# A second filter spectrum folded on VectorE out of PSUM, products on VectorE alone, GELU buffers by product slice and q in small loads

## The chip, the cores and the metric

The kernel runs on one core of a Trainium2 chip. A core has five engines with a queue each, and each works through its queue in the order written: TensorE (PE; its weight loads are shown apart as PEld), VectorE (DVE), ScalarE (ACT), GpSimd (POOL) and SyncE (SP), which here issues all the DMA transfers. The metric is the device time of one execution in microseconds. Before the change it is 228.35 us, the median of 3 runs (228.15 to 230.0).

## The reference

Two blocks follow one another on 2048 rows of 512 features, in bf16. Block A is a gated long convolution along the rows, block B a local mix and an MLP.

```python
x = A_q
h  = x + _A_ref(_layernorm(x), A_k, A_v, A_shift_k, A_ssm_k, A_ssm_D)
h2 = h + _B_ref(_layernorm(h), B_w1, B_w2, B_w3, B_w4)

# A: kv = (4-tap causal filter of k) * v
#    y  = irfft(rfft(kv padded to 4096) * rfft(ssm_k padded to 4096))[:2048]
#    A  = q * (y + kv * ssm_D)
# B: h  = gelu(layernorm(x) @ w1); its four quarters shifted by -1, +1, -2, +2 rows; @ w2
#    x1 = x + that;  B = x1 + gelu(layernorm(x1) @ w3) @ w4
```

## The kernel before

The convolution is done as a transform of 4096 points on TensorE, in two halves of 1024 rows. Signals are F0 and F1 (the filter's first half, and the whole filter for the second half of the rows) and A0 and A1 (the two halves of kv). The kernel is a list of small tasks. Each is made with `add(name, ...)` and knows its operands; a table `ORDER` (line 30) was written by a planner and says for each task its place, its engine (letter P, V, A, G or S) and the buffers it takes. `Plan.emit` (line 85) walks through the table, so each engine's queue is in the table's order. A wait at the head of a queue holds all that is behind it.

The tasks that matter, with their lines (S, h and p stand for a half, a part and a pair of row blocks):

- K, KV (lines 456, 457): the 4-tap filter on TensorE with diagonal matrices `dg` made of the taps, then times v out of PSUM on VectorE (L449).
- S1, E1, X (line 403): the forward transform's first step (L397), its eviction out of PSUM as a cast of 1024 columns (L266) and eight exchanges through SBUF to SBUF DMAs (L412). F1 sums two sources in PSUM, `fb` (the filter's second half) and `f0` (its first half with another table, `f1b`).
- S2, E2 (line 424): the second step (L420) and its eviction, the spectrum. E2 is a cast of 1024 columns on ScalarE or VectorE.
- P, I2, EV, XI (line 464): four or eight products for each of four slices `kl` of a half (L473, 1024 columns, two SBUF inputs), on VectorE or GpSimd, with four buffers; the inverse step (L485), its eviction and exchange (L495). The second half takes A0 x F1 and A1 x F0.
- I1 (line 499): the last inverse step (L503).
- Q, QN (lines 507, 516): mean and variance of q's rows (L512, L513), the reciprocal root as a power on GpSimd.
- Y, H, HS (line 580): normalised q, h (L591), h's statistics. uw, rr, hn (line 598) turn them into scale and bias.
- hb, LT, TE, W, U (line 653): normalised h, its transposition on TensorE or by two DMAs (`BYDMA`; a write and a DMA transpose), times w1 (L672), GELU (L676).
- X2, S, SS, R (line 683): the shifted product with w2 (L701), x1 (L704), its statistics, the rest (L708).
- lb, LX, EX, M, G, O, Z, OUT (line 715): normalised x1, transposition, times w3 (L752), GELU (L756), times w4 (L765), sum (L767) and store.

The GELU's outputs have three buffers `gb` (line 155) in memory of kv and of A1's spectrum. All G but those of the first pair of blocks wait for every product of A1 x F0 (line 759).

Of the kernel before, what the change touches and what calls it, by code (L numbers as in the profile page):

```python
# [9 lines left out]
P = 128  # L10
# [6 lines left out]
XW = 258  # L17

# [12 lines left out]
023V 004S 021P7 022P 055P01 001S 057P23 005S 061P45 006S 028V 029V 031V 032G 056A 008S 062A 058A 011S 059P67 060A 000S 024V 030A 091P10 033V 092V 002S  # L31
027V 003S 095P5 096V 083P41 034G 038V 039V 049P01 047P23 048A 035G 053P67 009S 050A 007S 054A 097P5 098V 093P3 014S 010S 084V 085P2 087P7 094V 040A
025A 109P01 036V 037A 086V 051P45 052A 089P6 017S 107P23 088V 111P45 041G 042V 043A 046G 067S 110V 108A 090V 045G 016S 070S 113P01 019S 114A 112V
099P67 103P23 104A 013S 101P45 102A 105P01 100V 063S 071P6723 072A 065S 073A 106V 333V 069S 211P50 212V 335V 064S 077P0167 079A 119S 026V 121S 078A
068S 115S 217P4 218V 123P2367 124V 125A 066S 080P0145 136V0 082A 135V1 116S 081A 213P7 120S 126P2345 127A 139G2 214V 128V 074P0167 076A 117S 015S 075V
138V3 129P2345 131A 130A 137P67010 122S 140P 012S 189P45 118S 177P23 141A 190A 179P67 337V 178A 018S 180A 175P45 176A 145V0 142V 143S 144V1 147V2
148V3 146P01231 149P 332V 151A 150A 183P67 153V0 020S 338V 181P45 182A 193S 192S 184V 336V 154G1 152S 156V2 185P23 186A 187P01 188A 132P4567 133A 194S
339V 157G3 334V 196S 219P31 134A 340G 191S 221P2 155P01450 158P 220V 044A 223P3 159A 222V 163V0 162V1 166V2 165V3 215P2 216V 160A 341G0 344G1 197S
164P67011 167P 168A 169V 229P45 224V 331G 195S 225P2 230A 226V 199P0167 200V 263V0 201A 233P45 234A 198S 241P23 161S 264G1 237P67 238A 235P01 236A
421V 170S 171P54 239P67 417V 242A 231P01 345V 232A 342V 347G0 240V 330S 422V 208P2345 343A 209A 172P10 210A 227P67 350G1 351V 356G1 173P32 348V 353G0  # L40
352V 228A 357V 346A 354V 365G 349A 174P54 362V1 363V 205P0167 207A 247S 366G 243S 206A 249S 359V0 360V 202P2367 204A 203A 251P0167 252A 367V 368V0
371V1 244S 267V2 253A 248S 266V3 378G 379G 380G 245S 369P50 372P4 370A 373V 254P0123 255V 256A 246S 381G0 265P67450 268P 384G1 364A 361A 257P0123 258A
269V0 259A 270V1 272V2 271P 382P11 385P0 403G 327S 273V3 274P 404G 405G 383A 328S 276A 374P3 275A 279V0 358A 250S 278V1 386V 375A 376P2 282V2 377A
355A 391G 407V0 392G 281V3 280P01451 283P 260P6723 409S 393G 261A 406V1 285V0 284V1 287V2 277S 288V3 286P 262A 408S 410S0 294V0 289P 290A 389P7 390A
293V1 387P6 295P01230 297V2 296V3 291A 298P 394V0 396S 395V1 397S 388A 299V0 413P7 414A 300V1 411P6 412A 302V2 303V3 301P 419V 304P 501P7 292S 306A
305A 309V0 308V1 502V 497P6 498V 503A 499A 311V2 561G 312V3 398S0 401P5 402A 420V 399P7 310P01231 314V0 313P 315V1 317V2 562G 400A 307S 563G 564A0
567A1 505P7 506V 507A 509P6 318G3 510V 418V 517P5 565P40 566V 513P7 568P6 569A 316P 329S 319P 511V 590G 320A 415V 591G 321A 570P60 571A 514V 416V 423G
592V 593A0 580P4 322S 595S 594A1 596S 515A 581A 576P7 597S1 582P3 574P6 583A 577A 424A0 578P2 572P1 573A 575A 579A 518V 519V 427G1 618G 504V 323P54
428V 324P73 325P10 429A 425V 426A 433G1 434V 619G 439G0 440V 430A1 435A 431V 620G 622A0 624S 326P64 598P51 604P3 599A 610P2 611A 445V0 446V 500V 448G
587P0 441A 436A1 432V 449G 450G 454A0 608P7 437V 588V0 438A 602P2 603A 584P5 621G1 623S 451A1 452P40 473V 474G 475G 453A 455P2 456A 606P1 607A 600P4  # L50
457P2 442G0 601A 625S0 476V1 478S 477V0 479S 480S1 461G 462G 463G 443V 464G1 447V 459P6 605A 465V0 609A 467S 466S 444A 626P40 468S0 632P7 458A 512V
636P3 638P2 485V 486G 460A 521P6 522V 523V 585V1 586S 525P1 639A 487G 488G0 489A1 628P2 481P6 629A 526V 527V 469P0 470A 646V 483P5 484A 630P2 631A
647G 637A 471P1 648V 650A0 649G1 615P5 490S 491S 492S1 495P0 493P3 472A 482A 541P6 494A 537P1 538V 540V 496A 529P3 530V 634P2 545P1 542V 543A 549P3
550V 633A 539A 674G 533P0 627A 553P6 524V 589S 534V 546V 535V 651S 544V 652S 531V 675G 653S1 730V 654P72 731G 612P4 658P3 732V 676G 551A 733G0 554V
547V 702V 735S 734V1 656P1 659A 616V0 528V 557P0 655A 660P3 661A 558V 662P7 677V0 664P6 635A 643P5 736S 737S0 520V 640P0 738P31 657A 536V 679S 665A
666P6 678G1 680S 559A 617S 703G 552V 663A 746P7 747A 704G 706G0 532V 708S 744P2 681S1 555A 644V0 645S 508V 740P5 748P7 758V 759G 760G 613V1 614S 742P1
516V 667A 761V0 682P60 745A 690P4 684P2 683A 705V1 707S 743A 686P6 685A 560V 694P1 762G1 671P2 672V0 673S 741A 750P5 641V1 687A 688P6 689A 764S 739A
691A 695A 668P2 692P6 749A 693A 709S0 710P42 556V 712P3 711A 722P7 763S 751A 765S1 752P6 755P5 716P4 766P11 713A 776P3 642S 777A 778P0 779A 753V0 754S
756V1 757S 699P6 718P5 669V0 670S 772P0 774P3 767A 773A 768P2 775A 770P1 771A 720P3 723A 548V 714P0 696P7 700V0 701S 697V0 769A 783P2 784V1 780P1 785S
698S 781V1 782S 721A 715A 717A 719A 727P7 728V0 729S 724P6 725V1 726S  # L60
# [3 lines left out]
class Plan:  # L64
# [4 lines left out]
    def add(self, name, opts, fn, deps=(), take=(), drop=(), size=0, mode=0, port=""):  # L69
        n = len(self.t)  # L70
        t = dict(n=n, name=name, opts=opts, fn=fn, deps=set(), take=list(take), drop=[], size=size, mode=mode, port=port)
        for d in deps:
            t["deps"].add(self.by[d])
        for d, part, *kind in drop:
            m = self.by[d]
            t["deps"].add(m)
            t["drop"].append((m, kind[0] if kind else self.t[m]["take"][0][0], part))
        self.by[name] = n
        self.t.append(t)
# [5 lines left out]
    def emit(self):  # L85
        for word in ORDER.split():
            t, slots, i = self.t[int(word[:3])], [int(c) for c in word[4:]], 0
            t["eng"], t["got"] = word[3], {}
            for kind, k in t["take"]:
                k = k if k > 0 else -2 * k  # L90
                t["got"][kind] = slots[i:i + k]
                i += k
            t["fn"](word[3], t["got"].get("ps", slots))
# [3 lines left out]
def body(ctx, tc, fx, kt, q, v, sk, sd, w1, w2, w3, w4, out):  # L97
# [20 lines left out]
    r_k = raw("r_k", 2 * DC * NB * 129)  # L118
# [12 lines left out]
    kT = r_k[:].rearrange("p (s c b x) -> p s c b x", s=2, c=DC, b=NB)  # L131
# [23 lines left out]
    gb = [view(r, lo, GS, "p (f x) -> p f x", f=FC) for r, lo in ((r_kv, 0), (r_x, 0), (r_x, GS))]  # L155
# [3 lines left out]
    wup = r_vs[:, 0:D]  # L159
# [4 lines left out]
    f1 = ct("f1", 2, 8, 2, 2, 2, 4)  # L164
# [8 lines left out]
    qst = ct("qst", 4, 6, dt=F32)  # L173
# [14 lines left out]
    ssk = ct("ssk", DC * 4)  # L188
# [15 lines left out]
    vec, pool, act = nc.vector, nc.gpsimd, nc.scalar  # L204
    vec.memset(negpi[:], -3.1415925)
# [3 lines left out]
    u1a, u1b = early(64), [early(64) for i in range(2)]  # L209
# [4 lines left out]
    vec.memset(wup, 0.0)  # L214
# [5 lines left out]
    s1 = early(128, BF16)  # L220
    mk = small("mk", 4, F32)

    def f1u(x):
        vec.scalar_tensor_tensor(out=u1b[x], in0=u1a, scalar=nf[:, 0:1], in1=u1b[x], op0=MUL, op1=ADD)
        vec.tensor_scalar(out=u1b[x], in0=u1b[x], scalar1=4095, scalar2=None, op0=AND)

    def f1s(x):
        act.activation(s1[:, 64 * x:64 * x + 64], u1b[x], ACT.Sin, bias=negpi[:], scale=SC)

    def f1m(x):  # L230
        for i in range(2):
            for j in range(2):
                vec.tensor_scalar(out=f1[:, x, :, i, :, j, :], in0=s1[:, 64 * x:64 * x + 64].rearrange("p (a c k) -> p a c k", a=8, c=2),
                                  scalar1=mk[:, 2 * i + j:2 * i + j + 1], scalar2=None, op0=MUL)
    f1u(0)
    f1s(0)
    vec.tensor_scalar(out=mk[:], in0=l4[:], scalar1=nf[:, 1:2], scalar2=None, op0=OP.is_equal)
    f1m(0)
# [3 lines left out]
    pool.iota(u1b[1].rearrange("p (a c k) -> p a c k", a=8, c=2), pattern=[[0, 8], [1024, 2], [0, 4]], base=2048, channel_multiplier=0)  # L242
# [7 lines left out]
    wf = small("wf", 72, F32)[:].rearrange("p (o b) -> p o b", o=9)  # L250
# [14 lines left out]
    def copy(e, o, i):  # L265
        (act.copy if e == A else vec.tensor_copy)(o, i)  # L266

    def pair(sl, k=0):
        return ps[:, sl[2 * k]:sl[2 * k] + 2, :]
# [12 lines left out]
    for c in range(DC):  # L282
        load(("Lk", 0, c), kT[:, 0, c], kt_r[0, c], size=258)
# [531 lines left out]
```

## Time and profile before

| what | value |
|---|---|
| median of 3 runs | 228.35 us |
| the profiled execution's own time | 229.05 us |
| its span (first to last instruction) | 227.3 us |
| PE busy | 203.9 us, 90% |
| PEld busy | 119.4 us, 53% |
| DVE busy | 142.3 us, 63% |
| ACT busy | 133.9 us, 59% |
| POOL busy | 85.6 us, 38% |
| mean granted TensorE clock | 0.977 |
| DMA | 34.49 MB, mean 152 GB/s |

A share is a mean over the whole span. The kernel has an early part (transforms, products) and a late part (matmuls with w1 to w4), and each view is to be read for them apart. In a list in order of time a line gives the start, the time it took, the engine, the line of the code, the operation with output and inputs, how often it comes in a row, and in brackets how long the engine was idle before and what ended that.

### The profile page before, as it was taken

How to read it: one execution, taken by the hardware profiler on the slowest of the kernel's cores; microseconds unless marked ns; L12 is line 12 of the kernel's file. 1: busy time of each engine (PE TensorE's matmuls, PEld its weight loads, DVE VectorE, ACT ScalarE, POOL GpSimd, SP SyncE). 2: the span in 40 equal slices, each digit the busy share in tenths (PEclk: the TensorE clock that was granted, in tenths of full speed). 3: DMA queues.
4: the chain of work that ended last, by engine and by line, in shares of the span. 5: the costliest groups of instructions: out<-in, count | busy, mean ns of one | idle time of the engine just before them, and what ended most of it. 6: DMA issues, size and time to landing. Idle time of an engine off the chain costs nothing.

```text
span 227.3 us, 5985 instructions
## 1 busy us (share of the span) xinstructions
PE 203.9 (90%) x2403; PEld 119.4 (53%) x2421; DVE 142.3 (63%) x309; ACT 133.9 (59%) x213; POOL 85.6 (38%) x210
## 2 busy tenths in 40 slices
PE   7998669998687965999999999899999999999993
PEld 2453224463123523556765877556668666667441
DVE  7789899899999888399484543088935030410221
ACT  4789868997799974458986747242505243037000
POOL 8724020846378774057685742005432100000000
PEclk9999997999997999699999999999999999999999
DMA  5999985698949144474522362700434053200021
GB/s 175 337 419 385 334 279 195 215 350 280 337 157 335 69 141 92 143 252 169 151 57 44 77 140 72 154 8 0 108 80 113 5 115 69 72 23 0 3 69 46
DMA packets 35229, 34.49 MB, mean 152 GB/s; under 512 B 26753, under 2 KB 28802, under 8 KB 34690
## 3 DMA queue, kind: packets, MB, share of 16 engines
q1 hardware_dynamic: 35202, 34.11, 46.8%
q8 instruction: 19, 0.31, 0.6%
q14 instruction: 8, 0.07, 0.1%
HBM read 13.13 MB, written 5.24 MB: 81 GB/s over the span
## 4 chain that ended last, share of the span: by engine, by line
PE 51%; ACT 7%; DMA 7%; DVE 6%; POOL 3%; issue 2%; DVEq 0%; ACTq 0%; SPq 0%; POOLq 0%
PE ps L765 20%; PE ps L752 19%; PE ps L701 5%; PE ps L672 4%; DMA hnT<-dhb 3%; ACT r_f L266 2%; DVE r_p L473 2%; PE ps L485 2%; ACT junk L575 2%; DMA r_dg<-dlb 1%; DMA dhb<-hbt 1%; ACT r_x L266 1%; DMA dlb<-r_k 1%; ACT r_k L625 1%; DVE r_kv L449 1%
## 5 line engine op out<-in xcount | busy, mean ns | idle before, releaser
L752 PE MATMUL ps<-r_dg,r_k 128*128 128x256 bf16 x448 | 51.5, 273 | 0.2 <-DMA r_dg<-dlb 0.2
L752 PEld LDWEIGHTS <-r_k 128*128 128x128 bf16 x448 | 43.6, 98 | 8.3 <-DMA r_dg<-dlb 0.7
L756 ACT ACTIVATE r_x<-ps 128x512 bf16<-128x512 f32 x35 | 19.5, 601 | 29.2 <-PE ps L752 29.2
L765 PE MATMUL ps<-w4s,r_x 128*128 128x512 bf16 x136 | 31.0, 379 | 0.2
L473 DVE TENSOR_TENSOR r_p<-r_a,r_f 128x1024 bf16<-128x1024 bf16 x28 | 23.4, 874 | 3.7 <-PE ps L485 3.6
L765 PEld LDWEIGHTS <-r_x 128*128 128x128 bf16 x140 | 13.7, 98 | 15.4
L485 PE MATMUL ps<-r_p,ttab 32*32 32x512 bf16 x768 | 18.3, 439 | 2.6 <-DVE r_p L473 2.5
L756 ACT ACTIVATE r_kv<-ps 128x512 bf16<-128x512 f32 x21 | 11.9, 604 | 12.8 <-PE ps L752 12.8
L672 PE MATMUL ps<-hnT,r_v 128*128 128x256 bf16 x128 | 16.0, 280 | 3.5 <-DMA hnT<-dhb 3.5
L765 PE MATMUL ps<-w4s,r_kv 128*128 128x512 bf16 x80 | 18.7, 379 | 0.2
L767 DVE TENSOR_TENSOR r_kv<-ps,r_a 128x512 bf16<-128x512 f32 x4 | 2.8, 692 | 24.7 <-PE ps L765 24.7
L266 ACT CAST r_y<-ps 128x1024 bf16<-128x1024 f32 x18 | 17.3, 1025 | 0.7 <-PE ps L397 0.7
L266 ACT CAST r_x<-ps 128x1024 bf16<-128x1024 f32 x15 | 14.5, 1020 | 4.5 <-PE ps L397 3.4
L473 POOL TENSOR_TENSOR r_p<-r_a,r_f 128x1024 bf16<-128x1024 bf16 x4 | 8.9, 2239 | 20.0 <-PE ps L485 10.7
L266 ACT CAST r_vs<-ps 128x1024 bf16<-128x1024 f32 x14 | 13.7, 1017 | 4.1 <-PE ps L485 4.1
L672 PEld LDWEIGHTS <-r_v 128*128 128x128 bf16 x128 | 12.5, 100 | 6.8 <-DMA hnT<-dhb 3.1
L397 PEld LDWEIGHTS <-f 128*32 128x32 bf16 x320 | 8.5, 101 | 13.3 <-issue 6.1
L441 PE MATMUL ps<-r_dg,r_k 128*128 128x256 bf16 (+3 forms) x107 | 14.7, 284 | 0.6 <-issue 0.3
L676 ACT ACTIVATE r_h<-ps 128x512 bf16<-128x512 f32 x16 | 9.1, 606 | 9.9 <-PE ps L672 9.9
L701 PE MATMUL ps<-r_v,r_h 128*128 128x512 bf16 x59 | 14.6, 380 | 0.3
L266 ACT CAST r_f<-ps 128x1024 bf16<-128x1024 f32 x14 | 13.3, 1016 | 2.2 <-PE ps L420 1.9
L485 PEld LDWEIGHTS <-ttab 32*32 32x32 bf16 x768 | 8.6, 90 | 10.7 <-issue 8.8
(165 smaller groups left out, 330.3 us busy)
## 6 DMA issues: line engine op xcount, KB each, us to landing
r_k<-in_kt_dram SPq DMA_DIRECT2D x8, 258.0 KB, 6.6
r_v<-in_v_dram SPq DMA_DIRECT2D x4, 512.0 KB, 7.0
r_f<-r_x SPq DMA_DIRECT2D x8, 256.0 KB, 3.8
r_q<-in_q_dram SPq DMA_DIRECT2D x2, 1024.0 KB, 7.4
r_a<-r_y SPq DMA_DIRECT2D x8, 256.0 KB, 3.7
r_x<-r_vs SPq DMA_DIRECT2D x4, 512.0 KB, 3.8
r_f<-r_y SPq DMA_DIRECT2D x8, 256.0 KB, 4.7
r_x<-r_y SPq DMA_DIRECT2D x8, 256.0 KB, 2.4
```

Source lines behind the costliest of these rows:

```text
L266: (act.copy if e == A else vec.tensor_copy)(o, i)
L397: nc.tensor.matmul(ps[32 * j:32 * j + 32, sl[hh], :], lhsT=f1t[:, i, 4 * t + 2 * hp + hh, :], rhs=src(2 * b + b0), start=(i == 0), stop=(i ...
L441: nc.tensor.matmul(o[:, (d + j0) * P:(d + j1 + 1) * P], lhsT=kT[:, s, c, bb, x:x + P], rhs=diag[:, c, j0:j1 + 1, :].rearrange("p j x -> p ...
L473: on[e].tensor_tensor(out=prs[:, sl[0], :, :], in0=sp[a][:, kl, t, :, :], in1=gv, op=MUL)
L485: nc.tensor.matmul(ps[c:c + 32, bk[h], :], lhsT=ttab[32 * h:32 * h + 32, 2 * kl + t, 2 if x else xx, 32 * b0:32 * b0 + 32], rhs=prs[32 * h ...
L575: act.activation(junk[:], x, ACT.Square, accum_out=sq[:, i, 1:2])
L672: nc.tensor.matmul(ps[:, sl[0], j * 256:(j + 1) * 256], lhsT=w1s[:, k, m * P:(m + 1) * P], rhs=hnT[:, k_, k, :], start=(k == 0), stop=(k = ...
L676: act.activation(h1T[:, 2 * h:2 * h + 2, 2 * p:2 * p + 2, 1 + P * s:1 + P * s + P], ps[:, got(("W", s, p, h))[0], :].rearrange("p (j b x) ...
L701: nc.tensor.matmul(ps[:, sl[0], :], lhsT=h1T[:, m, bb, x:x + P], rhs=w2s[:, m, :], start=(m == 0), stop=(m == DC - 1))
L752: nc.tensor.matmul(ps[:, sl[0], j * 256:(j + 1) * 256], lhsT=w3s[:, k, fc * P:(fc + 1) * P], rhs=lnT[:, k_, k, :], start=(k == 0), stop=(k ...
L756: act.activation(gb[got(("M", s, p, 0), "gb")[0]][:, 2 * fp:2 * fp + 2, :], ps[:, got(("M", s, p, fp))[0], :].rearrange("p (j x) -> p j x" ...
L765: nc.tensor.matmul(ps[:, sl[0], :], lhsT=gb[k_][:, fc, (b % 2) * P:(b % 2 + 1) * P], rhs=w4s[:, fc, :], start=(fc == 0), stop=(fc == FC - 1))
```

## The change

1. F1's first step takes the second half of the filter alone (`fb`), with the same table as F0. The first half's part is added at the spectrum: a task E2 of F1 is no longer a cast but two VectorE instructions, which add F0's spectrum, real and imaginary parts swapped, to what is in PSUM. The second table (`f1u`, `f1s`, `f1b`) is gone. F1 is loaded in four pieces.
2. Products are on VectorE alone.
3. Four GELU buffers `gb0` to `gb3`, each for two of the eight pairs, in memory of kv, A1's spectrum, and F0's and F1's. G of the pairs 1 to 3 waits for the products of one or two slices `kl`, G of the first for A1's first step, and the rest for none of these.
4. q comes in eight loads of 256 KB instead of two of 1 MB. A row's statistics keep the two partial results of L512; the aggregation (L513) is replaced by seven small instructions for eight blocks (QV), then the power (QP, GpSimd) and two instructions (QN).
5. A cast may be wide: marked M in the table, one ScalarE instruction evicts 2048 columns for two tasks. Three are.
6. The taps come with k, four columns behind each block of 1032; their own load is gone and each `dg` waits for its block of k.
7. The warm-up is twenty matmuls of 128 columns instead of five of 512. Planner costs and sizes are other numbers, and the table ORDER is written anew.

On the engines this gives, before to after: products on GpSimd 5 to 0; E2 of F1 on ScalarE 7 to 0 and on VectorE 1 to 8; hb on VectorE 9 to 4, ScalarE 3 to 9, GpSimd 4 to 3; Y on GpSimd 10 to 12, VectorE 3 to 0, ScalarE 3 to 4; `ftv` from GpSimd to VectorE. In TensorE's order W(0,0,1) stands ahead of S2(F1,1) and of the first I2 of the second half. In VectorE's order all eight Q of the second half stand behind its last product (before, three of them did). In SP's order the first half's four q loads stand ahead of all X(F0).

```diff
@@ emit
+        skip = False
         for word in ORDER.split():
...
-            t["fn"](word[3], t["got"].get("ps", slots))
+            if not skip:
+                t["fn"](word[3], t["got"].get("ps", slots))
+            skip = word[3] == "M"
@@ body: buffers
-    gb = [view(r, lo, GS, "p (f x) -> p f x", f=FC) for r, lo in ((r_kv, 0), (r_x, 0), (r_x, GS))]
+    gbq = [[view(r, lo, 2048, "p (f x) -> p f x", f=8) for lo in (0, 2048)] for r in (r_kv, r_x, r_f0, r_f1)]
+
+    def gb(i, f, n=1):
+        u = f // 8
+        r, z = ((0, u), (1 + u, 0), (1 + u, 1), (3, u))[i]
+        return gbq[r][z][:, f % 8:f % 8 + n, :]
@@ loads
-    load(("Lf", 1), fxs[:, 1, :, :].rearrange("p (g b) d -> p g b d", g=4), fx[1].rearrange("g p (b d) -> p g b d", b=2), size=1024)
+    for b in range(4):
+        load(("Lf", 1, b), fxs[:, 1, 2 * b:2 * b + 2, :], fx[1, b].rearrange("p (b d) -> p b d", b=2), size=310)
...
-        load(("Lq", s), q_sb[:, s], q_r[:, s], size=1024)
+        for g in range(4):
+            load(("Lq", s, g), q_sb[:, s, 2 * g:2 * g + 2, :], q_r[:, s, 2 * g:2 * g + 2, :], size=310)
...
-    add("skf", {V: 0.2}, lambda e, sl: vec.tensor_copy(sskf[:], ssk[:]), ["Lsk"])
+    for c in range(DC):
+        add(("skf", c), {V: 0.17, GP: 0.22, A: 0.22}, lambda e, sl, c=c: copy(e, sskf[:, 4 * c:4 * c + 4], kw[:, 0, c, NB * 129:KW]), [("Lk", 0, c)])
@@ forward2
+                if sig == "F1":
+                    def fold(e, sl, n=n, kl=kl, t=t):
+                        for r, op in ((0, SUB), (1, ADD)):
+                            vec.tensor_tensor(out=sp[sig][:, kl, t, r, :], in0=ps[:, got(n)[2 * t + r], :], in1=sp["F0"][:, kl, t, 1 - r, :], op=op)
+                    add(("E2", sig, kl, t), {V: 1.2}, fold, [("E2", "F0", kl, t)], drop=[(n, t)])
+                    continue
@@ conv
-                        add(("P", s, kl, i, x, t), {V: 0.605, GP: 2.4}, f, [("E2", a, kl, t), ("E2", g, kl, t), "f2", "f1b"] + before, take=[("pr", 1)], port="VG")
+                        add(("P", s, kl, i, x, t), {V: 0.605}, f, [("E2", a, kl, t), ("E2", g, kl, t), "f2"] + before, take=[("pr", 1)], port="VG")
@@ statistics of q
     def qstat(s, b):
...
-            vec.bn_stats(qst[:, i % 4, :], x)
-            vec.bn_aggr(qmv[:, i, :], qst[:, i % 4, :])
+        return lambda e, sl: vec.bn_stats(qst[:, 8 * s + b, :], q_sb[:, s, b, :])
+
+    def qvar(s):
...
+            en.tensor_tensor(out=qnm[:, i], in0=m0, in1=m1, op=ADD)
+            en.tensor_tensor(out=qrs[:, i], in0=m0, in1=m1, op=SUB)
+            en.tensor_tensor(out=qsd[:, i], in0=v0, in1=v1, op=ADD)
...
+    def qpow(s):
+        i = slice(8 * s, 8 * s + 8)
+        return lambda e, sl: pool.tensor_tensor(out=qrs[:, i], in0=qsd[:, i], in1=mhalf[:], op=OP.pow)
@@ F1's sources
-    forward1("F1", [fb, f0], lambda b: ["f1b", ("Lf", 1)] + [("Lf", 0, i) for i in range(4)] + ["dr"], lambda b: [("X", "A0", b // 2, kl) for kl in range(4)])
+    forward1("F1", fb, lambda b: ["f1", ("Lf", 1, b)], lambda b: [("X", "A0", b // 2, kl) for kl in range(4)])
@@ back
-            gd = [("S1", "A1", b, hp) for b in range(4) for hp in range(2)] + (allp(1) if g else [])
+            gd = [] if g >= 4 else [("S1", "A1", b, hp) for b in range(4) for hp in range(2)] if g == 0 else [x for kl in range((1, 2, 2)[g - 1]) for x in allkl(kl)]
```

## The prediction

> **What bounds the kernel now.** I read the stretches of ten microseconds first, because two engines change places as the bound. Columns: stretch, its length, then busy us (and instructions) of PE, PEld, DVE, ACT, POOL, then TensorE clock, DMA share, GB/s.
>
> ```profile
> 20.00:30.00 10.00, 7.21 (x116) 3.04 (x117) 8.89 (x14) 8.60 (x11) 2.74 (x3) 1.00 0.94 349
> 50.00:60.00 10.00, 8.63 (x163) 3.43 (x163) 9.60 (x13) 8.07 (x10) 5.89 (x9) 1.00 0.84 289
> 60.00:70.00 10.00, 6.81 (x96) 2.16 (x91) 9.73 (x27) 9.00 (x14) 6.19 (x17) 1.00 0.62 248
> ...
> 160.00:170.00 10.00, 9.95 (x66) 6.27 (x65) 6.80 (x13) 3.27 (x7) 4.68 (x5) 1.00 0.39 93
> 200.00:210.00 10.00, 9.95 (x75) 7.23 (x74) 0.69 (x1) 4.94 (x11) 0.00 (x0) 1.00 0.04 13
> ```
>
> Early, VectorE is 89 to 97% busy and TensorE has holes; late, TensorE has none. The border is the last product of the second half and its matmuls (I2). TensorE in order of time (start, us, engine, line, operation):
>
> ```profile
> 36.01 4.07 PE L397 MATMUL ps<-r_h,f 128*32 128x512 bf16 x64
> 41.12 3.64 PE L397 MATMUL ps<-r_h,f 128*32 128x512 bf16 x64
> ...
> 104.26 1.14 PE L485 MATMUL ps<-r_p,ttab 32*32 32x512 bf16 x64
> 105.33 6.29 PE L752 MATMUL ps<-r_dg,r_k 128*128 128x256 bf16 x56
> ```
>
> From 105 us to the last matmul's end (223.6, the chain of waits) the five-microsecond stretches leave TensorE only 1.5 us idle. Before 104.26 it is idle some 18 us. In both orders exactly the same tasks stand behind the last I2: 56 M, 16 O, 8 W, 10 X2, 4 I1, 2 LT. So **the end is the start of the last I2 plus about 119.4 us** (223.63 - 104.26), and I forecast that start.
>
> What sets it is VectorE's queue of some 100 us. Its order of time, beside GpSimd's, shows what is hidden there:
>
> ```profile
> 28.02 3.21 DVE L473 TENSOR_TENSOR r_p<-r_a,r_f 128x1024 bf16<-128x1024 bf16 x2
> 40.86 2.63 DVE L473 TENSOR_TENSOR r_p<-r_a,r_f 128x1024 bf16<-128x1024 bf16 x1 [0.81 <-PE ps L485]
> 49.59 2.49 DVE L473 TENSOR_TENSOR r_p<-r_a,r_f 128x1024 bf16<-128x1024 bf16 x4
> 56.57 2.19 DVE L473 TENSOR_TENSOR r_p<-r_a,r_f 128x1024 bf16<-128x1024 bf16 x1
> ```
> ```profile
> 27.96 2.12 POOL L473 TENSOR_TENSOR r_p<-r_a,r_f 128x1024 bf16<-128x1024 bf16 x1 [7.26 <-DMA r_a<-r_y]
> 40.81 4.66 POOL L473 TENSOR_TENSOR r_p<-r_a,r_f 128x1024 bf16<-128x1024 bf16 x2 [10.73 <-PE ps L485]
> 56.09 2.13 POOL L473 TENSOR_TENSOR r_p<-r_a,r_f 128x1024 bf16<-128x1024 bf16 x1 [1.98 <-ACT r_f L266]
> 101.99 2.13 POOL L473 TENSOR_TENSOR r_p<-r_x,r_f 128x1024 bf16<-128x1024 bf16 x1
> ```
>
> Four products in a row take 2.49, so 0.62 each. A product beside one of GpSimd's takes far more: 3.21 - 1.24 = 1.97, 2.63 - 0.62 = 2.01, 2.19 - 0.62 = 1.57 too much. **GpSimd's products cost VectorE 5.5 us** in its full stretch. The fifth, at 101.99, is late by itself: VectorE's own last product ends at 101.55, and the I2 waits until 104.26.
>
> **What the Trainium skill says.** "SBUF — State Buffer", Who interferes with whom: a VectorE instruction with two SBUF inputs contends with a GpSimd instruction that reads SBUF, and the second to issue blocks fully. The trace agrees (2.63 against 0.62). It adds that an instruction with one SBUF input does not contend. Here too: a sum of L704 (one input SBUF, one PSUM) at 102.13 beside the GpSimd product takes 0.74, its usual 0.741. So the new fold, PSUM with one SBUF input, is outside the conflict. "VectorE: DVE Perf Modes", The perf-mode tier table: a tensor_tensor that reads PSUM runs at the 1x rate; L449's 512 columns out of PSUM take 0.682, as long as 1024 SBUF columns in L473 (0.684): the fold's rows are dear.
>
> **The change part by part**, VectorE up to the last product, at start-to-start durations of its order of time:
>
> - Products: five more at 0.62 = +3.1; conflict -5.5.
> - Fold: eight evictions of F1's spectrum, seven of them ScalarE's (0.91 to 0.94 each in its rows of four), become 16 VectorE additions. L449's pair took 1.28 and the next operation began 1.19 after its start, so 0.60 each: 8 x 1.19 = 9.5, less one old VectorE cast of 1.13: +8.4. ScalarE loses 7 x 0.92 = 6.4, its chain of 61 to 74 us in the chain of waits.
> - Statistics of q: L512 with L513 takes 0.83, without the aggregate 0.61 at most. 13 blocks stood ahead of the last product, now 8 (the other half's are moved behind it): 8 x 0.61 - 13 x 0.83 = -5.9. Their later cost is 8 x 0.61 and the joint seven small operations, about 6 us behind the last I2; seven M cover them (6.3 us) and three I1 (2.7), before TensorE's first O, so I count nothing; uncovered, up to 2 us.
> - Tables: the second one of the forward step falls (0.45 + 0.58): -1.0. The table product ftv comes from GpSimd: +1.1.
> - Reassigned, ahead of the last product: hb 6 to 2 at 0.34, -1.4; one HS -0.8; two Y -1.1; two TE -0.7; one S +0.7; one uw +0.5. Casts other than F1's last step stay at 11, KV at 16.
>
> Sum without the conflict +2.9, with it **-2.6**: the last VectorE product moves from 101.55 to 98.9, if VectorE idles as long as before (12.4 us up to there). As the fifth GpSimd product is gone too, the last I2 starts at about 99.0: **-5.2**.
>
> TensorE must allow it. F1's forward step has half its matmuls: (4.07 + 3.64)/2 = 3.9 us less, at 36 to 45 us where TensorE is 100% busy and VectorE waits for it (0.81). Its work before the last I2 is then 104.3 - 18 - 3.9 = 82.4 us, so at 99.0 it idles 16.6: feasible. The shorter warm-up (five 512-column matmuls, 2.31 us) is hidden by the first load of fx: nothing.
>
> ScalarE: -6.4 by the fold, about +5 by hb, one diag and Y. Three wide evictions join two casts of 1024 columns each: 0.53 from start to start for 512 columns (L756) and 0.93 for 1024 leave a fixed 0.13, so that is what one saves. Net about -1 over the kernel, and it isn't last in the late part.
>
> DMA: q in eight 256 KB loads instead of two of 1 MB, F1's half in four. Same bytes, nine more issues of 0.6 us in SP's queue less one of the taps. SP waits there for other engines, so 0; but the first half's q is now moved ahead of all the F0 exchanges, 1.0 MB at about 400 GB/s = 2.5 us earlier in a DMA stretch that is full (share 1.01 at 10 to 20 us). F0's last exchanges were held by ScalarE's casts until 17.91, so this is covered unless the loads run past 18. The taps arrive with k: diag waits for a 258 KB load (6.6 us to landing against 2.3), and ftv stands ahead of KV in VectorE's queue, so A0's path (KV, cast, exchange, S2) is later: **+1.0**, between 0 and 2.5.
>
> GELU buffers: M's gate on all products, now by slice, costs 0 either way: no ScalarE wait at L756 ends on VectorE, all end on PE.
>
> Sum: -5.2 + 1.0 = **-4.2**. The profiled execution took 229.05 (span 227.3 and 1.75 around it), so 224.85; against the median of 228.35, which is what is asked, **224.2**.
>
> **Rivals.**
> (a) *Holes close too.* VectorE's 12.4 idle us are mostly waits for TensorE (2.83 at 94.17, while TensorE waits 2.77 for a DMA transpose of hb); with W spread out and four hb on ScalarE, 4 of them vanish: 220.
> (b) *New order, new waits.* The front gains, but transposed inputs come late: one OUT stands in SP's queue ahead of block pair 4's write, and I work out a slack of 2 us only. Gain 1: 227.4. For it: TensorE waited for such transposes three times before (2.77, 0.71, 0.19).
> (c) *Slower: the folds stand last in line.* W(0,0,1) is put ahead of S2(F1,1) and of all second-half I2 in TensorE's queue. W waits for ScalarE (hb, transpose eviction), ScalarE for GpSimd's power, that for H. In the old trace H ended at 61.88 and the transposed block at 72.5, 10.6 us. In the new order I count 11 us of VectorE work from H to the fold of slice 1 and about 12 for the chain. Each us of lateness beyond goes to folds, products and I2 alike: from 4.2 us on the kernel is slower; at 7 it is 231.2. Against it: this chain had ScalarE's F1 evictions in it (four of 0.92), which go.
> (d) *The conflict stays*, as GpSimd's eight Y (0.76, one SBUF input) and statistics block VectorE's products: then the last product ends at 101.55 + 2.9 = 104.5 instead of 104.1, and with the taps' 1.0 it is 229.7. Four products beside a GpSimd hb took 2.92 against 2.49, so only 0.4 a time.
>
> **How the numbers follow.** Forecast (223 to 226) 0.46; (a) 0.22; (b) 0.14; (c) 0.11; (d) 0.07. One per cent, about what a measurement of this kernel can tell, is 2.3 us. Faster by over 1% (below 226.07): forecast, (a), a fifth of (b) = 0.71. Slower (above 230.63): (c) nearly whole and some of (d) = 0.12. The rest 0.17. The range 219.3 to 229.0 leaves out (c), some of (d) and the far end of (a); the taps' bounds (0 to 2.5) and the uncovered statistics (2) lie inside.
>
> **What would show it.** Right: no L473 row on POOL and no product of VectorE over about 1 us; the last I2 near 100; TensorE's idle after it at most 3 us; the F1 step at 3.8 us. The fold wrong if its additions take over 0.75. Wrong altogether if the last I2 starts after 104, or if the later part holds over 4 us of TensorE waits on transposes.

## The result, and the profile after

The changed kernel takes 220.86 us in the median of 4 runs (219.75 to 222.94), against 228.35 for the kernel before beside it: a ratio of 0.967, interval 0.958 to 0.975. Repeated with the first experiments it was 222.29, ratio 0.977 (0.965 to 0.988), so the gain is 5 to 8 us. The profiled execution took 222.94 us, 6.1 less than the one before; its span is 221.2 us at a mean clock of 0.974. Some executions are 1.5 to 3.3 per cent slower than the fastest of their kernel, mostly at a lower granted clock: the ratios here leave these out, the medians do not, and of the traces only r2's (230.36 us) is of such a one.

The stretches of ten microseconds of the changed kernel, columns as in the prediction:

```profile
50.00:60.00 10.00, 7.08 (x84) 2.22 (x86) 8.02 (x14) 6.17 (x7) 2.97 (x7) 0.83 1.00 364
60.00:70.00 10.00, 6.64 (x82) 2.82 (x79) 8.96 (x25) 9.41 (x21) 7.86 (x17) 0.81 0.47 173
70.00:80.00 10.00, 8.44 (x192) 4.21 (x190) 8.88 (x16) 8.60 (x13) 6.06 (x19) 0.84 0.59 196
80.00:90.00 10.00, 9.84 (x258) 5.16 (x256) 9.69 (x17) 9.21 (x14) 2.51 (x6) 1.00 0.55 137
...
160.00:170.00 10.00, 10.00 (x94) 8.95 (x93) 7.04 (x17) 5.38 (x10) 3.51 (x6) 1.00 0.44 104
200.00:210.00 10.00, 10.00 (x64) 6.07 (x63) 1.39 (x2) 2.99 (x6) 0.00 (x0) 1.00 0.12 39
```

The same stretch of the kernel before, from 80 to 90 us:

```profile
80.00:90.00 10.00, 5.78 (x192) 3.19 (x191) 8.77 (x17) 6.67 (x12) 6.03 (x15) 1.00 0.42 113
```

Two things are new. From 50 to 60 us VectorE is no longer full (8.02 against 9.60), although the fold is there. And TensorE's large holes end at 80 us: it is busy 9.84 and then 9.54 of ten (90 to 100), where before it was busy 5.78 from 80 to 90. Its order of time around the last I2:

```profile
99.04 1.14 PE L493 MATMUL ps<-r_p,ttab 32*32 32x512 bf16 x64
100.11 6.29 PE L781 MATMUL ps<-r_dg,r_k 128*128 128x256 bf16 x56
```

The last I2 starts at 99.04 (104.26 before), and the last matmul ends 118.4 us later, at 217.5, in place of 119.4. So the early part gives 5.2 of the 6.1 us. The other 0.9 lies behind the last I2, where TensorE idled 1.5 us before and does not idle now: all five-microsecond stretches from 100 to 215 us are full.

VectorE's order of time shows the fold (L432), the last products (L481) and the moved statistics (L516):

```profile
51.12 3.68 DVE L432 TENSOR_TENSOR r_f<-ps,r_f 128x512 bf16<-128x512 f32 x6
...
93.44 2.50 DVE L481 TENSOR_TENSOR r_p<-r_a,r_f 128x1024 bf16<-128x1024 bf16 x4 [0.94 <-PE ps L493]
96.52 2.50 DVE L481 TENSOR_TENSOR r_p<-r_x,r_f 128x1024 bf16<-128x1024 bf16 x4
99.60 4.84 DVE L516 BATCH_NORM_STATS2 qst<-r_q 128x6 f32<-128x512 bf16 x8
```

An addition takes 0.60 from start to start, four products take 2.50, no product stands on GpSimd or takes over 1 us, and eight statistics take 0.61 each. These prices of the prediction hold. F1's first step, which comes in five pieces, takes 4.4 us for its 64 matmuls, where 3.8 was named. It doesn't follow that the sum of the prices explains the gain: the experiments say that part of it does not.

### The profile page after: what moved, and what is told of

The parts are those of the page before. It is cut to its first block, busy times and chain, and to the rows that moved or that the text cites. A ratio compares the mean times of both kernels' runs of the same rounds, so it can differ in the third digit from the quotient of the medians.

```text
span 221.2 us, 5913 instructions
## 1 busy us (share of the span) xinstructions
PE 200.6 (91%) x2372; PEld 118.7 (54%) x2372; DVE 145.3 (66%) x320; ACT 134.9 (61%) x214; POOL 67.3 (30%) x187
## 4 chain that ended last, share of the span: by engine, by line
PE 67%; DMA 11%; SPq 6%; ACT 6%; DVE 5%; issue 2%; POOL 0%; DVEq 0%
PE ps L781 22%; PE ps L793 22%; PE ps L729 6%; PE ps L700 5%; PE ps L493 4%; SPq L412 4%; DMA r_h<-in_fx_dram 3%; SPq L275 3%; DMA r_k<-in_kt_dram 3%; DMA r_x<-r_y 3%; PE ps L511 3%; DVE r_f L432 2%; PE ps L397 2%; ACT r_y L266 2%; DMA r_f<-r_y 2%
## 5 line engine op out<-in xcount | busy, mean ns | idle before, releaser
L781 PEld LDWEIGHTS <-r_k 128*128 128x128 bf16 x448 | 43.6, 98 | 7.8 <-issue 0.7
L785 ACT ACTIVATE r_f<-ps 128x512 bf16<-128x512 f32 x26 | 14.9, 598 | 27.8 <-PE ps L781 27.8
L793 PE MATMUL ps<-w4s,r_f 128*128 128x512 bf16 x104 | 24.1, 379 | 0.0
L481 DVE TENSOR_TENSOR r_p<-r_a,r_f 128x1024 bf16<-128x1024 bf16 x32 | 20.8, 694 | 1.0 <-PE ps L493 0.9
L795 DVE TENSOR_TENSOR r_kv<-ps,r_v 128x512 bf16<-128x512 f32 x5 | 3.4, 686 | 20.5 <-PE ps L793 20.5
L785 ACT ACTIVATE r_x<-ps 128x512 bf16<-128x512 f32 x16 | 9.2, 599 | 12.2 <-PE ps L781 12.2
L793 PEld LDWEIGHTS <-r_f 128*128 128x128 bf16 x104 | 10.2, 98 | 11.8
L266 ACT CAST r_vs<-ps 128x1024 bf16<-128x1024 f32 (+1 forms) x12 | 14.3, 1228 | 2.4 <-PE ps L493 1.9
L793 PE MATMUL ps<-w4s,r_x 128*128 128x512 bf16 x64 | 15.1, 379 | 0.0
L449 PEld LDWEIGHTS <-r_k 128*128 128x128 bf16 x112 | 9.5, 98 | 8.9 <-issue 4.6
L793 PE MATMUL ps<-w4s,r_kv 128*128 128x512 bf16 x56 | 12.6, 379 | 0.0
```

The source lines that it names most:

```text
L266: (act.copy if e in "AM" else on[e].tensor_copy)(o, i)
L449: nc.tensor.matmul(o[:, (d + j0) * P:(d + j1 + 1) * P], lhsT=kT[s][c][:, bb, x:x + P], rhs=diag[:, c, j0:j1 + 1, :].rearrange("p j x -> p ...
L481: on[e].tensor_tensor(out=prs[:, sl[0], :, :], in0=sp[a][:, kl, t, :, :], in1=gv, op=MUL)
L781: nc.tensor.matmul(ps[:, sl[0], j * 256:(j + 1) * 256], lhsT=w3s[:, k, fc * P:(fc + 1) * P], rhs=lnT[:, k_, k, :], start=(k == 0), stop=(k ...
L785: act.activation(gb(gi, 2 * fp, 2), ps[:, got(("M", s, p, fp))[0], :].rearrange("p (j x) -> p j x", j=2), ACT.Gelu_apprx_tanh)
L793: nc.tensor.matmul(ps[:, sl[0], :], lhsT=gb(gi, fc)[:, 0, (b % 2) * P:(b % 2 + 1) * P], rhs=w4s[:, fc, :], start=(fc == 0), stop=(fc == FC ...
```

## The experiments

All kernels, with the engine that evicts F1's spectrum ("fold" where the addition is done there), in the order of the instructions of before ("old") or of the changed kernel ("new"). The ratio is to the kernel before, run beside each. The last I2 is read from one execution of each: two executions of the changed kernel have it at 99.04 and 98.55, after being 1.8 us apart at the first S2 of A0 (27.95 and 26.11), so half a microsecond there tells nothing.

| kernel | order | F1's spectrum | last I2 | median us | ratio (interval) |
|---|---|---|---|---|---|
| before | old | ScalarE 7, VectorE 1 | 104.26 | 228.35 | 1 |
| r3, products moved | old | ScalarE 7, VectorE 1 | 100.47 | 225.70 | 0.989 (0.981 to 0.997) |
| r12, and cast on VectorE | old | VectorE | 109.27 | 233.24 | 1.026 (1.017 to 1.035) |
| r6, and fold | old | VectorE, fold | 113.24 | 237.58 | 1.050 (1.038 to 1.061) |
| r5, fold alone | old | VectorE, fold | 114.36 | 240.09 | 1.057 (1.044 to 1.070) |
| r10, r6 with VectorE relieved | old | VectorE, fold | 108.79 | 237.92 | 1.054 (1.044 to 1.065) |
| r4, no fold | new | ScalarE 7, VectorE 1 | 105.27 | 229.35 | 1.008 (1.005 to 1.012) |
| r9, no fold, cast on VectorE | new | VectorE | 98.59 | 223.66 | 0.988 (0.973 to 1.004) |
| r1, changed | new | VectorE, fold | 98.55 | 222.29 | 0.977 (0.965 to 0.988) |
| r2, five products on GpSimd | new | VectorE, fold | 105.54 | 228.91 | 1.000 (0.996 to 1.004) |
| r7, q's statistics early | new | VectorE, fold | 97.64 | 222.85 | 0.981 (0.965 to 0.996) |
| r8, taps by themselves | new | VectorE, fold | 98.36 | 223.42 | 0.984 (0.972 to 0.996) |
| r11, q in two loads | new | VectorE, fold | 99.47 | 223.15 | 0.986 (0.982 to 0.991) |

### The products (r1, r2, r3)

The theory was that VectorE's queue up to the last product sets the last I2, the rival that GpSimd's products cost little and the fold or the order brings the gain. First the changed kernel as it is:

> The changed kernel again, as the yardstick of this group. VectorE's queue theory (the end is the start of the last I2 plus about 119 us): 219 to 222 us, ratio to before 0.96 to 0.97, last I2 within 1 us of 99.0. If the first runs were lucky, the ratio is over 0.975.

Then the changed kernel with five products put back, in the letters of its order:

```diff
-147V3 ... 162V1 ... 165V2 ... 272V1 ... 326V3
+147G3 ... 162G1 ... 165G2 ... 272G1 ... 326G3
```

> The changed kernel with the same five products on GpSimd as before the change. Queue theory: VectorE saves 5 x 0.62 = 3.1 but loses up to 2.0 beside each of them, and the last I2 waits for a GpSimd product (2.1 instead of 0.6): 2 to 5 us slower than the changed kernel, VectorE products of 2 us or more in the trace. Rival (the gain is the new order of tasks, not the conflict): within 1 us of the changed kernel.

And the kernel before with the same five moved to VectorE:

```diff
-139G2 ... 154G1 ... 157G3 ... 264G1 ... 318G3
+139V2 ... 154V1 ... 157V3 ... 264V1 ... 318V3
```

> The kernel before, with only its five GpSimd products moved to VectorE, same places in the order. Queue theory: -5.5 + 3.1 on VectorE and the last product no longer late: 2.4 to 5 us faster than before, 223.5 to 226. Rival (order): VectorE only gets 3.1 us more work, 228 or slower.

r3 gains 2.4 us (228.1 in its own comparison to 225.7), which is the size of the prediction's -5.5 + 3.1; in the ratio's interval it is 0.8 to 4.3. r2 loses 6.6 us against r1 by the medians and 5.3 by the ratios, more than expected. Its trace is of an execution 1.5 us above its median, so the trace shows where the loss arises rather than how large it is. GpSimd's and then VectorE's order of time in r2, and what TensorE waited for (us in total, times, longest):

```profile
44.12 0.58 POOL L524 TENSOR_TENSOR qnm<-qst 128x8 f32<-128x8 f32 x1 [1.83 <-DVE qst L516]
...
45.16 0.73 POOL L528 TENSOR_SCALAR qmv<-qnm 128x8 f32<-128x8 f32 x1
...
47.14 2.12 POOL L481 TENSOR_TENSOR r_p<-r_a,r_f 128x1024 bf16<-128x1024 bf16 x1
```

```profile
40.33 2.50 DVE L481 TENSOR_TENSOR r_p<-r_a,r_f 128x1024 bf16<-128x1024 bf16 x1
...
50.50 1.30 DVE L481 TENSOR_TENSOR r_p<-r_a,r_f 128x1024 bf16<-128x1024 bf16 x2 [4.07 <-PE ps L493]
```

```profile
PE ps L493 <- POOL r_p L481: 4.2, 1, 4.2
```

The conflict is there (one product takes 2.50 in place of 0.62), but the loss starts with a wait. In the new order GpSimd has the small operations of q's variance, which start only when VectorE's statistics are done (44.12), and the product queued behind them comes at 47.14. I2 waits 4.2 us for it, and VectorE 4.07 for I2's release of a product buffer. This I2 still starts when r1's does (43.46 against 43.32), behind the product of 2.50; the next one starts at 54.79 against 47.17, and the last is 7.0 late. Besides the wait, fourteen matmuls of K behind it take 3.60 us for 1.92 in r1, at a clock of 0.50 from 50 to 55 us. So with these five products on GpSimd, in these places, the new order and the fold together are worth nothing.

### The fold in the new order (r4, r9)

r4 is the changed kernel with F1 made from both sources again and its spectrum cast, 7 of 8 on ScalarE as before; r9 differs from r4 in the engine of seven casts alone. Against the changed kernel it gives TensorE 64 matmuls more in F1's first step, and makes the second table again (about 1 us on VectorE). The diff is r4's; r9 keeps the letters V of the last line but one.

```diff
-    forward1("F1", fb, lambda b: ["f1", ("Lf", 1, b)], ...
+    forward1("F1", [fb, f0], lambda b: ["f1", ("Lf", 1, b)], ...
...
-                if sig == "F1":
+                if sig == "none":
...
-... 208V ... 209V ... 217V ... 218V ... 215V ... 214V ... 212V 211V
+... 208V ... 209A ... 217A ... 218A ... 215A ... 214A ... 212A 211A
```

> The changed kernel without the fold: F1's first step sums both sources as before and its spectrum is cast, by ScalarE in seven of eight. VectorE 7.4 us less, ScalarE 6.4 more where it is 90% busy, TensorE 3.9 more. Queue theory with all three engines: 0 to 2 us slower than the changed kernel. If VectorE alone set the front: up to 7 us faster. Rival (the fold itself is a gain, by halving TensorE's step): 4 us slower or more.

> The changed kernel without the fold (F1 from the blocks of both halves, twice the matmuls in its first step, as in before), but with the evictions of F1's second step cast on VectorE, in the very places where the changed kernel folds there, so that VectorE's and ScalarE's queues are as long as in the changed kernel and only TensorE has 3.9 us more. If the run without the fold was slow because its casts came back to ScalarE: within 1.5 us of the changed kernel, last I2 at 98.5 to 100. If what the fold saves is TensorE's matmuls: 3 to 6 us slower than the changed kernel, last I2 at 102 to 105.

Stretches of five microseconds of r4:

```profile
65.00:70.00 5.00, 1.45 (x24) 0.47 (x19) 4.93 (x15) 4.94 (x11) 4.24 (x11) 0.82 0.46 175
70.00:75.00 5.00, 4.59 (x48) 2.14 (x48) 1.39 (x3) 4.86 (x11) 1.89 (x5) 0.50 0.93 312
75.00:80.00 5.00, 2.03 (x55) 0.91 (x40) 0.62 (x2) 4.76 (x8) 2.85 (x11) 0.84 0.26 95
```

and of r9:

```profile
65.00:70.00 5.00, 3.94 (x32) 2.03 (x32) 5.00 (x9) 4.59 (x9) 3.06 (x11) 0.52 0.90 318
70.00:75.00 5.00, 4.39 (x97) 1.51 (x104) 3.78 (x6) 4.56 (x8) 2.73 (x11) 0.50 0.56 186
75.00:80.00 5.00, 4.85 (x118) 2.90 (x103) 5.00 (x9) 4.15 (x6) 4.30 (x10) 0.96 0.28 57
```

In r4 ScalarE (fourth number) is full, 14.6 of 15 us, while VectorE works 2.0 of the last ten and TensorE 8.1 of the fifteen. The first two casts that moved back show how it comes about, in r4 and then in r9:

```profile
54.40 1.91 ACT L275 CAST r_f<-ps 128x1024 bf16<-128x1024 f32 x2
57.27 1.24 PE L407 MATMUL ps<-r_kv,f 128*32 128x512 bf16 x16 [2.32 <-ACT r_y L275]
79.38 1.29 DVE L492 TENSOR_TENSOR r_p<-r_x,r_f 128x1024 bf16<-128x1024 bf16 x2 [8.00 <-ACT hbt L664]
```

```profile
54.08 1.05 PE L407 MATMUL ps<-r_kv,f 128*32 128x512 bf16 x16 [0.49 <-ACT r_y L275]
```

They hold the cast of A1's first step behind them on ScalarE, and TensorE waits 2.32 us for it. VectorE, which has no cast there, waits 8.00 us for ScalarE, up to 79.38. With the seven casts on VectorE, TensorE does 13.2 of the fifteen and the last I2 comes 6.7 us earlier, as early as with the fold. Of these 6.7, 1.4 are there already at A0's last S2 (41.02 against 39.66), ahead of the first cast that moved, so some 5.3 go with the casts. The clock is no rival: it is low in these stretches of both (0.82, 0.50, 0.84 and 0.52, 0.50, 0.96).

From r4 to r9 it is 5.7 us by the medians and 2.0% (4.5 us) by the ratios, whose intervals just part. The prediction's cost of the fold to VectorE is thus true and without effect here, and **what pays is that the evictions leave ScalarE**. The halved matmuls don't show: last I2 at 98.59 against 98.55, spans of 220.7 both. Up to there r9's TensorE works 85.0 us and idles 13.6, r1's works 83.0 and idles 15.6. The medians differ by 1.4 us and the ratios by 1.2% (2.7 us) with intervals that overlap, so a gain of the fold's own up to about that size is not excluded.

### The fold in the old order (r5, r6, r12)

```diff
-    forward1("F1", [fb, f0], lambda b: ["f1b", ("Lf", 1)] + [("Lf", 0, i) for i in range(4)] + ["dr"], ...
+    forward1("F1", [fb], lambda b: ["f1", ("Lf", 1)], ...
...
+                if sig == "F1":
+                    def fold(e, sl, n=n, kl=kl, t=t): ...
...
-200V ... 201A ... 209A ... 210A ... 207A ... 206A ... 204A 203A
+200V ... 201V ... 209V ... 210V ... 207V ... 206V ... 204V 203V
```

r5 is this, without the second table; r6 has the five products on VectorE as well, and r12 has only the letters of the last two lines together with the products.

> The kernel before with the fold alone: F1 is multiplied from the second half's blocks only (half the matmuls of its S1 groups), and the evictions of its second step add F0's spectrum out of PSUM on VectorE in the places where they were cast (7 of 8 casts leave ScalarE); the scaled copies of the first half's blocks are left out; the five products stay on GpSimd, and the order of the instructions, the loads and the Q statistics stay as before. VectorE-queue theory (the fold is VectorE's 7 to 8 us more ahead of the last product, little of it given back): last I2 at 107 to 109, 3 to 5 us slower than before. ScalarE theory (between 60 and 80 us TensorE waits for ScalarE's evictions, VectorE is half idle there, so the fold takes work off the bound): 2 to 4 us faster, with the waits of the D groups and of X for ScalarE shorter.

> The kernel before with the fold and the five products on VectorE, in the order of before, with its Q statistics, loads and buffers. If these two parts make up nearly all of the change: 5 to 7 us faster than before, last I2 at 98 to 101. If the new order of the instructions and the Q statistics carry the rest: less than 3.5 us faster, last I2 after 101.

> The order of before with the five products on VectorE and without the fold (F1 from the blocks of both halves), but with all eight evictions of F1's second step cast on VectorE, where the order of before gives ScalarE seven of them. If the fold failed in the old order because of the engine that its evictions are on: as slow as the run with the fold and the products, 236 to 240 us, last I2 at 112 to 115. If it failed because of something of the fold itself (its reading of F0's spectrum, the changed lengths of F1's first step): near the run with the products alone, within 3 us of 225.7, last I2 at 100 to 103.

Both theories of r5 fell: it is 11 us slower, not 3 to 5 slower or 2 to 4 faster, and r6 is 9 slower where either case had it faster. r12 lies between its two cases: the engine of the evictions alone costs 7.5 us (225.70 to 233.24; by the ratios 3.7%, 8.4 us), the fold on top of it another 4.3 (by the ratios 5.4). What TensorE waits for in r12:

```profile
PE ps L420 <- DVE r_f L266: 4.5, 2, 2.7
PE ps L397 <- DVE r_f L266: 2.3, 1, 2.3
```

and its stretches:

```profile
65.00:70.00 5.00, 2.50 (x32) 0.71 (x29) 4.86 (x13) 1.36 (x5) 3.44 (x9) 1.00 0.76 297
70.00:75.00 5.00, 1.75 (x24) 0.43 (x27) 4.96 (x9) 0.00 (x0) 3.32 (x12) 0.62 0.84 280
```

The kernel before in the same stretches:

```profile
65.00:70.00 5.00, 3.12 (x56) 0.87 (x50) 4.80 (x16) 4.97 (x9) 4.29 (x15) 1.00 0.70 271
70.00:75.00 5.00, 4.42 (x108) 1.97 (x104) 4.75 (x11) 4.95 (x9) 4.10 (x8) 0.66 0.96 309
```

This is r4 turned round. In the old order VectorE and ScalarE were both full from 65 to 75 us (9.55 and 9.92 of ten). With the evictions moved, ScalarE idles there, VectorE is full, and TensorE waits for banks of PSUM that VectorE has yet to empty. Of the 4.3 us of the fold itself no experiment here tells the cause. In the traces 1.8 of the 4.0 us by which r6's last I2 is later are there at 31 us (S2 of F0 at 31.52 against 29.72), before the first fold.

### Relieving VectorE in the old order (r10)

```diff
-421V ... 417V ... 422V ... 240V ... 352V ... 359V0 ... 362V1 ... 371V1
+... 240A ... 352A ... 359A0 ... 362A1 ... 371A1 ... 416V 422V 417V 421V
```

> The order of before with the fold and the five products on VectorE, and VectorE relieved between the first fold and the products behind the last one: three Q statistics of the second half (2.6 us) go behind the last product, and a cast of A1 (1.2), a statistic of H (0.9), two steps of z (1.1) and one of hb (0.4) go to ScalarE, which idled 8 us in that stretch of the run with the fold in the old order: 6.1 us of VectorE in all. If the fold failed in the old order because it lengthened VectorE's queue there: 4 to 7 us faster than that run (about 231 to 234), last I2 at 106 to 109. If the place of the fold in TensorE's and the DMA's order is what it lacks: less than 2 us faster, last I2 after 111.

The last I2 comes 4.5 us earlier than in r6 (108.79 against 113.24), as the theory of the queue has it, but the median doesn't move (237.92 against 237.58). The two traces are no fair pair: r6's execution took 239.46 us, 1.9 above its median, and r10's 236.86, 1.1 below. Nor is the last I2 back at r3's 100.47. So whether VectorE's 6.1 us of other work are part of the reason stays open, and they are not all of it. The relief made waits of its own: VectorE waits 1.42 us for a z that is now ScalarE's, with a fold queued behind (at 67.58), and behind the last I2 an I1 waits 1.26 us for a GELU. Which other moves of the new order are needed stays open.

### Q's statistics, the taps, q's loads (r7, r8, r11)

r7 puts five of the eight statistics that the change moved behind the last product back ahead of it:

```diff
-271V0 ... 275V3 ... 305V3 ... 311V3 ... 319V3 ... 425V ... 426V ... 427V ... 428V ... 429V
+271V0 425V ... 275V3 426V ... 305V3 427V ... 311V3 428V ... 319V3 429V
```

> The changed kernel with five of the eight Q statistics of the second half put back ahead of the last products on VectorE (one after each of P(1,0,0,0,0), P(1,0,0,1,1), P(1,2,0,1,1), P(1,2,1,1,1), P(1,3,0,1,0)), some 5 x 0.61 = 3 us. Queue theory (VectorE runs without slack up to the last product from 80 us on): last I2 3 us later, kernel 2.5 to 3.5 us slower than the changed one. If the 11 us in which VectorE idles ahead of the last product lie between these places, or something other than VectorE sets the last I2: 0 to 1 us.

The last I2 doesn't come 3 us later; it stands at 97.64. What VectorE waited for from 70 to 105 us, in the changed kernel (r1) and in r7:

```profile
DVE r_p L481 <- PE ps L493: 1.8, 2, 1.5
```

```profile
DVE r_p L482 <- PE ps L494: 0.5, 1, 0.5
```

The statistics went partly into time in which VectorE waited for TensorE to free product buffers. TensorE waits for little from 75 us on (0.6 us and 0.3 for ScalarE in r7), so by this reading the end of the early part in the changed kernel is TensorE's own.

r8 gives the taps their own small load:

```diff
+    ssk = ct("ssk", DC * 4)
...
-        load(("Lk", 0, c), kw[:, 0, c, :], kt[0, c], size=300)
+        add(("Lk", 0, c), {SP: 0.6}, lambda e, sl, c=c: ([nc.sync.dma_start(ssk[:], sk)] if c == 0 else [], nc.sync.dma_start(kw[:, 0, c, :], kt[0, c])), size=300)
...
-        add(("skf", c), ..., copy(e, sskf[:, 4 * c:4 * c + 4], kw[:, 0, c, NB * 129:KW]), [("Lk", 0, c)])
+        add(("skf", c), ..., copy(e, sskf[:, 4 * c:4 * c + 4], ssk[:, 4 * c:4 * c + 4]), [("Lk", 0, c)])
```

> The changed kernel with the shift taps in a small load of their own ahead of k's first load, where the changed kernel takes them out of the columns behind k. If the first D group waits for the taps behind the load of k, its first KV comes some 2 us earlier (8.8 to 9.3 in place of 11.1) and the kernel is 1 to 2 us faster. If TensorE and VectorE take the delay up before the first products: KV early, the kernel within 0.7 us.

KV does not come earlier, although the taps do (their copy is at 5.89, in r1 at 6.84). VectorE in r8:

```profile
11.77 2.00 DVE L458 TENSOR_TENSOR r_kv<-ps,r_v 128x512 bf16<-128x512 f32 x3 [1.43 <-DMA r_v<-in_v_dram]
```

It waits for v. SyncE's queue before and in r1 (start, time to issue) shows why:

```profile
3.07 0.43 SPq L272 DMA_DIRECT2D r_v<-in_v_dram  x1
```

```profile
4.79 1.56 SPq L275 DMA_DIRECT2D r_v<-in_v_dram  x2
```

In the new order four loads of fx and four of k stand ahead of v, before it was two of each. The later start of the front (first KV at 11.09 in the profiled execution and 11.47 in r1 against 8.76, first product at 30.95 and 29.43 against 28.02) isn't the taps' doing. By the queues it goes with the order of the loads, which no run changed, and what it costs in the end wasn't tried. r8's last I2 is as early as r1's; its median is 1.1 us higher, and behind the last I2 TensorE waits 1.9 us for a transpose by DMA, which r1 doesn't.

r11 loads q in two pieces of 1 MB:

```diff
-            load(("Lq", s, g), q_sb[:, s, 2 * g:2 * g + 2, :], q_r[:, s, 2 * g:2 * g + 2, :], size=310)
+            add(("Lq", s, g), {SP: 0.6}, lambda e, sl, s=s, g=g: nc.sync.dma_start(q_sb[:, s], q_r[:, s]) if g == 0 else None, size=310)
```

> The changed kernel with q loaded as before, in two loads of 1 MB in place of eight of 256 KB. Nothing waits for q in the traces of both kernels: within 0.7 us of the changed kernel. If the shorter loads let others pass: 1 to 2 us slower.

Last I2 at 99.47, a median 0.9 us above r1 and a ratio 1.0% (2.2 us) above it with overlapping intervals: a loss of 1 to 2 us is neither shown nor excluded.

## Why the prediction was right, and where not

The direction and the range hold: 220.86 us in 219.3 to 229.0. The gain was 7.5 us in the medians, 6.1 in the profiled executions and 5.4 by the ratio of the repetition, for 4.2. The last I2 came at 99.04; the prediction's queue sum has it at about 99.0, and with its 1.0 us for the taps at 100.0.

One line was misread. The prediction takes the end of GpSimd's fifth product (104.12) for what I2 at 104.26 waits for. But TensorE is busy up to that moment. The kernel before:

```profile
90.50 2.62 PE L672 MATMUL ps<-hnT,r_v 128*128 128x256 bf16 x16 [2.77 <-DMA hnT<-dhb]
...
103.94 0.39 PE L643 MATMUL ps<-ident,r_k 128*128 128x128 bf16 x4
```

and the changed one:

```profile
90.89 1.92 PE L700 MATMUL ps<-hnT,r_v 128*128 128x256 bf16 x16 [0.47 <-DMA hnT<-dhb]
```

From this wait for a transpose of hb on, TensorE is all but dense in both. The wait is over at 90.50 and 90.89, but 13.8 us pass from there to the last I2 before and 8.2 after: more of the work has been done by then. Up to the last I2 TensorE worked 86.0 us and idled 18.2 before, 82.2 and 16.9 after. By the prediction's steps:

- **End = last I2 + 119.4: right for the changed kernel**, with 118.4. To the end of the span it is 122.0 to 122.3 us in the changed kernel, r1, r4, r7, r9 and r11, and 123.0 to 123.3 in before, r2, r3 and r12. In r8 it is 124.1 (the transpose), in r5, r6 and r10 124.2 to 126.3. The 0.9 us that closed behind the last I2 was counted as nothing.
- **Conflict -5.5 and five products +3.1: right in size in the old order** (r3: -2.4). In the new order the same products cost 5 to 7 us, and a wait behind q's variance on GpSimd comes with them. Neither the forecast nor rival (d) had that.
- **Fold +8.4: the step that failed.** Its size was right (0.60 each), but it was entered as a cost, and the ScalarE time that it frees (6.4) as worth little, since "it isn't last in the late part". With the casts on ScalarE (r4), TensorE waits for it from 55 us on and it is full from 65 to 80. In the new order moving the evictions to VectorE gains 5.7 us (r4 to r9); in the old one it costs 7.5 (r3 to r12). A sum over 100 us of one queue can't show either sign: it adds time in a stretch where that engine may idle.
- **Q's statistics -5.9: without effect where it was tried.** Five of the moved eight back in place cost nothing (r7). The assumption that VectorE is last up to the last product is what fails here; from 75 us on TensorE is nearly dense.
- **The sum -2.6: right for the last product, not in its parts.** The last product ends 2.5 us earlier (101.55 to 99.02), but VectorE's work up to there fell by 1.1 only (89.1 to 88.0). The small operations on h's statistics take 2.5 us there, 0.4 before, for which the sum has 0.5. VectorE's idle time, which was to stay at 12.4, made up the rest with 11.1. Two errors met, and one term was charged and another credited that both didn't count, so the close hit is partly luck.
- **Rival (a), closing holes:** VectorE's closed by 1.4 us, TensorE's by 1.3 up to the last I2; TensorE's lie earlier now.
- **F1's step -3.9 on TensorE: feasible and idle**, as said: r9 has the matmuls back with the same last I2.
- **Taps +1.0: wrong cause.** The front starts 2.3 us later, and not through the taps (r8); the forecast's place for it is not where the end is set, as far as these runs tell.
- **q's loads 0: not contradicted** (r11). The warm-up and the GELU buffers were not tried apart; no wait in the trace points at them.
- **Rivals (b) and (c) did not come**: TensorE waits for no transpose behind the last I2. One wait of 2.2 us for ScalarE's hb stands at 67 us, on the path that (c) named; it stays below the 4.2 us from which (c) would decide.
- **The Trainium skill**, "SBUF — State Buffer", Who interferes with whom, says that a VectorE instruction with two SBUF inputs contends with a GpSimd one that reads SBUF. It is borne out again: a VectorE product beside GpSimd's takes 2.50 against 0.62 in r2.

Measured by pairs, the change is: products -2.4 (r3), and the rest -3.4 more (r3 to r1). Of this rest the evictions' engine and the new order don't work singly: new order with the evictions on ScalarE +3.7 (r3 to r4), evictions on VectorE in the old order +7.5 (r3 to r12). Both without the fold give -2.0 (r3 to r9), and what is left for the fold, -1.4, is inside the noise.

## What to carry to other kernels

When work moves between engines, price it by stretch: look at which of the two engines is full there and which idles, because the same seven evictions gained 5.7 us in one order and lost 7.5 in another. An order written out in advance fits one assignment of engines, so a part of such a change that is tried alone can show the wrong sign; test the pair and both halves. A sum that hits the measured value is not yet an explanation: take a term out and see whether the time moves. And two things that end and start together are not yet a wait: look whether the engine was idle in between.

## What was not expected of the hardware

Small GpSimd operations suffer beside VectorE's products too: in r2 operations on 128x8, of which others took 0.20 us, took 0.58 and 0.73 while a product ran. And the granted clock shows in short matmuls. In r1, in a stretch at full clock and in one where the clock granted was 0.50:

```profile
21.52 0.62 PE L420 MATMUL ps<-r_f,ftab 64*32 64x512 bf16 x16
70.49 1.05 PE L420 MATMUL ps<-r_f,ftab 64*32 64x512 bf16 x16
```

TensorE was not full just before the second (3.27 of five at 65 to 70 us).
